# Identity and zero multiplications inserted in TensorE's planned waits, in an attention and rational feed-forward kernel

## The chip, the cores and the metric

The kernel runs on one core of a Trainium2 chip. Its time is the device time of one execution, in microseconds. Before the change the median of three runs is 824.97 us (824.67 to 826.0). The engines are TensorE (PE, with its weight loads as PEld), VectorE (DVE), ScalarE (ACT), GpSimd (POOL), and SyncE (SP), which issues the transfers. [...]

## The reference

Two attention steps and a feed-forward block with a rational function between its two products:

```python
def sm_attn(qq, kk, vv):
    s = scale * np.matmul(qq, kk.transpose(0, 1, 3, 2))
    a = np.exp(s - np.max(s, axis=-1, keepdims=True))
    a = a / (np.sum(a, axis=-1, keepdims=True) + 1e-09)
    return np.matmul(a, vv)
p_packed = sm_attn(p, k, v)                    # 32 packed rows for each head
out = sm_attn(q, p_packed, p_packed)           # 8 x 8 heads, 576 rows, 64 wide
# x: 4608 x 512, the heads side by side
h = x @ w_in                                   # 512 -> 2048
P = a[0] + a[1]*h + a[2]*h**2 + a[3]*h**3
Q = 1.0 + abs(b[0])*abs(h) + abs(b[1])*h**2
out = (P / (Q + 1e-6)) @ w_out                 # 2048 -> 512
```

The weights w_in and w_out come in as 64-bit floats.

## The kernel before, in words

The kernel goes through eight batches of 576 tokens. For each batch `attention` transposes k, forms the scores of the packed rows (buffer `small`), their exponentials (`kx`) and the packed result (`ppT`), transposes q (also into `kx`), forms the second scores, and leaves the normalised weights as two float32r parts, `AH` and `AL`. `m_chunk` multiplies the packed result by w_in (`win`, float32; products in the banks `at`) and splits it into the high and low part `m`. `hidden` multiplies `m` with `AH` and `AL` into the two PSUM banks `h` (six steps of 288 columns for one block) and evaluates the rational function (`U`, `V`, `Y`); `gh` and `gl` are the parts of the result. `accumulate` multiplies them by the parts of w_out (`w`), in steps of 512 columns, into the PSUM banks `acc`.

The weights' 64-bit words have to be turned into float32 first. `convert` does it with two ScalarE passes (lines "m<-m", "w<-w", "win<-m" in the trace) and three VectorE passes per portion, 15 portions and two halves in all, in the first 140 us. While words are left (`early`), `m_chunk` casts its products on ScalarE and forms the low part through a further multiplication by the negative identity (`neg`, in buffer `full`; "m<-full" in the trace), so that VectorE is spared.

Nothing is issued as it is written. `Planner` (line 30) records every instruction with its engine and operands, prices it (`COST`, `F32`), and `schedule` makes a list schedule from the prices. `order` gives the sequence by planned start, and `issue` (line 212) hands the instructions to the engines in that sequence. Each engine then works strictly through its queue, waiting wherever an operand or a buffer isn't ready. Therefore the planned gaps on TensorE set the number of inserted multiplications, while the real gaps are those of the trace. The prices that matter are these:

```python
COST = {"vector": (70, 1.04), "scalar": (93, 0.83), "gpsimd": (215, 2.11), "tensor": (15, 0.417)}
TRANSPOSE, F32 = (15, 0.834), (30, 1.667)
```

They are ns for one instruction and ns for a column. The PSUM banks are two each for `acc`, `h`, `at` and `V`; during the first batch `attention` uses `acc` beside `at`.

Of the kernel before, what the change touches and what calls it, by code (L numbers as in the profile page):

```python
# [14 lines left out]
F32R = mybir.dt.float32r  # L15
# [4 lines left out]
ALU = mybir.AluOpType  # L20
# [3 lines left out]
P = 128  # L24
# [7 lines left out]
class Planner:  # L32
# [156 lines left out]
    def order(self):  # L189
        n = len(self.ops)  # L190
        self.costs = [self.price(*x) for x in self.ops]
        self.transfers = [self.transfer(calls[0][1]) if engine == "sync" else 0 for engine, calls in self.ops]
        before = self.edges()
        after = [[] for _ in range(n)]
        for i, x in enumerate(before):
            for j in x:
                after[j].append(i)
        sync = [x[0] == "sync" for x in self.ops]
        rank = list(range(n))
        best = None  # L200
        for r in range(self.ROUNDS):
            start, end = self.schedule(before, after, rank)
            if best is None or max(end) < best[0]:
                best = self.best = max(end), start, end
            s, e = self.schedule(after, before, [-x for x in end], True)
            m = max(end)
            rank = [m - x for x in e]
        self.t0 = best[1]; self.deps = dict(enumerate(before))
        self.end = best[0]
        return sorted(range(n), key=lambda i: (best[1][i], i))  # L210

    def issue(self):
        for i in self.order():
            engine, calls = self.ops[i]
            for name, args, kwargs in calls:
                getattr(getattr(self.nc, engine), name)(*args, **kwargs)  # L216

# [14 lines left out]
class Ring:  # L232
# [10 lines left out]
    def next(self, shape=None, dtype=None):  # L243
        return self.at(self.used % self.n, shape, dtype)
# [3 lines left out]
def attention_rational_ffn(  # L248
# [12 lines left out]
    B, H, T, D = q.shape  # L261
# [19 lines left out]
    sb = ctx.enter_context(tc.tile_pool(name="sb", bufs=1))  # L281
    ps = ctx.enter_context(tc.tile_pool(name="ps", bufs=1, space=PSUM))
    tc.nc.scalar.preload_act_table_set("natural_log_exp_and_others")
    nc = Planner(tc.nc)


    ident = sb.tile([P, P], F32, name="ident")
    make_identity(tc.nc, ident)
    ab, abS, one, root = (sb.tile([P, n], F32, name=x) for n, x in ((6, "ab"), (7, "abS"), (1, "one"), (5, "root")))
    win = sb.tile([P, NCH, NCC, CF], F32, name="win")  # L290
    G = sb.tile([P, NFC, 2 * REM], F32, name="G")
# [20 lines left out]
    gh_ring, gl_ring = (Ring(sb, x, 2, [P, 2, HMAIN], F32R) for x in ("gh", "gl"))  # L312
    acc_ring = Ring(ps, "acc", 2, [P, DM])
    h_ring = Ring(ps, "h", 2, [P, 512])
    V_ring = Ring(ps, "V", 1, [P, 2, 512])
    at_ring = Ring(ps, "at", 2, [P, 512])


    def constants():
        nc.vector.tensor_scalar(neg, ident, -1.0, None, ALU.mult)  # L320
        nc.sync.dma_start(ab[:, 0:4], a.rearrange("(o n) -> o n", o=1).broadcast_to([P, 4]))
        nc.sync.dma_start(ab[:, 4:6], b.rearrange("(o n) -> o n", o=1).broadcast_to([P, 2]))
        nc.vector.tensor_scalar(abS[:, 0:6], ab, S, None, ALU.mult)
        nc.vector.scalar_tensor_tensor(abS[:, 4:6], abS[:, 4:6], -1.0, abS[:, 4:6], ALU.mult, ALU.max)
        nc.vector.memset(one, (1.0 + 1e-6) * S)

        m, e, p, r, i = (root[:, n : n + 1] for n in range(5))
        nc.vector.scalar_tensor_tensor(m, ab[:, 5:6], -1.0, ab[:, 5:6], ALU.mult, ALU.max)
        nc.vector.tensor_scalar(m, m, 2.0**-126, None, ALU.max)
        nc.vector.tensor_scalar(e.bitcast(I32), m.bitcast(I32), 23, None, ALU.logical_shift_right)  # L330
        nc.vector.tensor_scalar(e.bitcast(I32), e.bitcast(I32), 127, None, ALU.add)
        nc.vector.tensor_scalar(p.bitcast(I32), e.bitcast(I32), 1, 23, ALU.logical_shift_right, ALU.logical_shift_left)
        nc.vector.reciprocal(i, p)
        nc.vector.tensor_scalar(m, m, i, i, ALU.mult, ALU.mult)
        nc.scalar.activation(r, m, AF.Ln)
        nc.scalar.activation(r, r, AF.Exp, scale=0.5)
        nc.vector.reciprocal(i, r)
        nc.vector.scalar_tensor_tensor(r, m, i, r, ALU.mult, ALU.add)
        nc.vector.tensor_scalar(abS[:, 6:7], r, p, 0.5 * S**0.5, ALU.mult, ALU.mult)
        for i, reg in enumerate((reg_a3, reg_b0, reg_b1, reg_root)):  # L340
            nc.scalar.reg_load(reg, abS[0:1, 3 + i : 4 + i].bitcast(I32))
# [8 lines left out]
    words = [("in", 2 * c, 2) for c in range(NCH)] + [("out", 2 * c, 2) for c in range(NCH - 1)]  # L350
# [298 lines left out]
    def m_chunk(bb, c, n=1):  # L649
        assert index["in", 2 * (c + n) - 1] < converted  # L650

        early = converted < len(words)
        f = slice(c % 2 * CF, (c % 2 + n) * CF)
        if c % 2 == 0:
            M[bb, c // 2] = m_ring.at(c // 2)
        m = [M[bb, c // 2][:, i] for i in range(2)]
        t = [at_ring.next()[:, 0 : n * CF] for _ in range(NG)]
        tiles(
            (
                (  # L660
                    t[r][32 * j : 32 * j + 32], PPT[bb][64 * r : 64 * r + 64, r, 32 * j : 32 * j + 32],
                    win[64 * r : 64 * r + 64, c : c + n, j, :],
                ),
                dict(start=True, stop=True),
            )
            for j in range(NJ)
            for r in range(NG)
        )
        for r in range(NG):
            mh, ml = (x[:, r, f] for x in m)  # L670
            if early:
                nc.scalar.copy(mh, t[r])
                nc.tensor.matmul(t[r], neg, mh, start=False, stop=True, skip_group_check=True)
                nc.scalar.copy(ml, t[r])
            else:
                split(t[r], mh, ml, nc.vector)
# [81 lines left out]
    def acc_block(u, i):  # L758
        bb, x, c = units[u]
        if c == 0 and i == 0:  # L760
            ACC[bb, x] = [acc_ring.next() for _ in range(2)]
        gh, gl = GS[bb, x, c]
        acc = ACC[bb, x][i]
        for f in range(2):
            cols = slice(i * P, (i + 1) * P)
            accumulate(acc, gh[:, f, cols], gl[:, f, cols], 2 * c + f, c == 0 and f == 0, c == NCH - 1 and f == 1)
        if c < NCH - 1:
            return
        if i == 0:
            O[bb, x] = o_ring.next()  # L770
        o = O[bb, x]
        ov = out[bb * T : bb * T + NS * P, :].rearrange("(p i x) m -> p x i m", i=2, x=2)[:, x]
        if u == NU - 1 and i == 1:
            nc.vector.tensor_copy(o[:, i, :], acc)
        else:
            nc.scalar.copy(o[:, i, :], acc)
        if u == NU - 1:
            nc.sync.dma_start(ov[:, i, :], o[:, i, :])
        elif i == 1:
            nc.sync.dma_start(ov, o)  # L780

    for what in ("k0", "rem", "k1", "v0", "v1", "q0", "q1"):
        load(0, what)
    constants()
    load_words(2)
    for _ in attention(0):
# [18 lines left out]
    for bb in range(1, B):  # L805
        gen = attention(bb)
        at = [u for u in range(2 * UB * bb - 30, 2 * UB * bb - 3) if u not in mt]
# [4 lines left out]
    def stage(u):  # L812
        if u in pipe:
            next(pipe[u])

    def filler(i):
        if i in mt:
            m_chunk(*mt[i])
        for x in fill.get(i, ()):
            next(x)  # L820

    for u in range(NU + LAG + 2):
        if u < NU:
            pipe[u] = hidden(*units[u])
        stage(u)
        if 0 <= u - LAG < NU:
            acc_block(u - LAG, 0)
        filler(2 * u)
        stage(u)
        stage(u - 2)  # L830
        stage(u - 1)
        for x in rem.get(u, ()):
            remainder(*x)
        convert()
        while converted < len(words) and due(words[converted]) <= u + 1:
            convert()
        if 0 <= u - LAG < NU:
            acc_block(u - LAG, 1)
        filler(2 * u + 1)
    with tc.manual_schedule():  # L840
        nc.issue()


# [26 lines left out]
```

## Time and profile before

| | us |
|---|---|
| median of three runs | 824.97 |
| profiled execution | 823.16 |
| its span, first to last instruction | 821.4 |
| TensorE busy in the span | 774.1 (94%) |
| VectorE busy | 693.6 (84%) |
| ScalarE busy | 691.5 (84%) |
| GpSimd busy | 460.9 (56%) |
| mean granted TensorE clock | 0.969 |

Read the shares by stage, since the averages mix two stages with different limits. The span is cut in 40 slices of some 20.5 us on the profile's page; the granted clock is below 0.9 only in slices 2 to 5 and 7. From about 147 us to the end TensorE is busy without a break. [...]

### The profile page before, as it was taken

Reading aid. Unit: us, or ns where it says so; the run is one execution under the profiler, and the core shown is the slowest. Engines: PE = TensorE matmul, PEld = TensorE weight load, DVE = VectorE, ACT = ScalarE, POOL = GpSimd, SP = SyncE. Lnnn points to the kernel's source line nnn. Section 1 sums busy time; section 2 is a strip of 40 time slices with the busy share of each in tenths; the row PEclk is TensorE's granted clock in tenths of the full one; section 3 lists DMA queues with packets and bytes.
Section 4 is the critical chain, followed back from the end, with each engine's and each line's share of the span. In section 5 each row is a group of like instructions: output and inputs, shape, how many; then the busy total and the mean of one; then the engine's idle time right before and its main releaser. Section 6 shows DMA issues by size and latency. Waiting matters only on the chain.

```text
span 821.4 us, 15529 instructions
## 1 busy us (share of the span) xinstructions
PE 774.1 (94%) x5584; PEld 613.7 (75%) x5584; DVE 693.6 (84%) x1296; ACT 691.5 (84%) x1566; POOL 460.9 (56%) x462
## 2 busy tenths in 40 slices
PE   5677788999999999999999999999999999999997
PEld 3355565888877877788877877788877878778886
DVE  2999999888898788988798778988798788998873
ACT  5898888899797879999888869999888889898872
POOL 0006455755487546755577445755578445856663
PEclk9678798999999999999999999999999999999999
DMA  8973241010400212010400203010400210000001
GB/s 250 387 253 105 104 123 27 26 57 26 123 27 1 81 50 87 27 52 31 123 26 1 81 20 117 27 52 30 123 27 1 77 37 31 26 1 27 26 2 39
DMA packets 50941, 56.06 MB, mean 68 GB/s; under 512 B 13488, under 2 KB 40112, under 8 KB 50864
## 3 DMA queue, kind: packets, MB, share of 16 engines
q1 hardware_dynamic: 50864, 55.07, 20.9%
q8 instruction: 44, 0.72, 0.4%
q14 instruction: 33, 0.27, 0.1%
HBM read 45.62 MB, written 9.44 MB: 67 GB/s over the span
## 4 chain that ended last, share of the span: by engine, by line
PE 75%; DVE 12%; ACT 7%; DMA 2%; issue 1%; SPq 1%; POOL 0%; DVEq 0%; ACTq 0%; POOLq 0%
PE acc L216 36%; PE h L216 23%; PE at L216 16%; DVE Y L216 5%; DVE small L216 3%; DMA m<-in_moe_w_in_dram 2%; DVE w L216 2%; ACT w L216 1%; ACT V L216 1%; ACT m L216 1%; DVE V L216 1%; ACT Y L216 1%; SPq L216 1%; ACT U L216 1%; ACT kx L216 1%
## 5 line engine op out<-in xcount | busy, mean ns | idle before, releaser
L216 PE MATMUL acc<-w,gh 128*128 128x512 f32 x1024 | 330.6, 401 | 4.4 <-ACT w L216 4.4
L216 PEld LDWEIGHTS acc<-w,gh 128*128 128x128 f32 x1024 | 186.6, 190 | 47.8 <-issue 5.8
L216 POOL TENSOR_TENSOR U<-U,sq 128x576 f32<-128x576 f32 x118 | 168.8, 1431 | 73.1 <-ACT U L216 31.6
L216 POOL TENSOR_TENSOR gl<-Y,gh 128x512 fp32r<-128x512 f32 x128 | 166.2, 1299 | 65.0 <-ACT gh L216 32.2
L216 PE MATMUL acc<-w,gl 128*128 128x512 f32 x512 | 198.4, 401 | 0.0
L216 PE MATMUL h<-AH,m 128*128 128x288 f32 x1024 | 193.6, 308 | 4.5 <-DVE Y L216 4.0
L216 PEld LDWEIGHTS h<-AH,m 128*128 128x128 f32 x1024 | 160.0, 192 | 36.2 <-DVE Y L216 16.9
L216 ACT ACTIVATE Y<-h,abS 128x288 f32<-128x288 f32 x256 | 128.2, 513 | 27.6 <-PE h L216 23.8
L216 DVE TENSOR_TENSOR Y<-Y,h 128x288 f32<-128x288 f32 x256 | 111.3, 447 | 40.0 <-ACT sq L216 20.0
L216 DVE SCALAR_TENSOR_TENSOR Y<-Y,abS,V 128x576 f32<-128x576 f32 x128 | 103.4, 808 | 39.3 <-ACT V L216 38.6
L216 DVE SCALAR_TENSOR_TENSOR Y<-Y,abS,h 128x288 f32<-128x288 f32 x256 | 126.4, 507 | 3.3
L216 ACT ACTIVATE sq<-h 128x288 f32<-128x288 f32 x236 | 98.3, 422 | 33.9 <-PE h L216 31.9
L216 PEld LDWEIGHTS acc<-w,gl 128*128 128x128 f32 x512 | 96.7, 190 | 28.4 <-issue 7.7
L216 PE MATMUL h<-AL,m 128*128 128x288 f32 x512 | 112.7, 300 | 0.0
L216 POOL COPY G<-Y 128x64 f32<-128x64 f32 x128 | 34.6, 270 | 135.9 <-DVE Y L216 102.9
L216 ACT ACTIVATE U<-h 128x288 f32<-128x288 f32 x256 | 100.9, 426 | 8.5 <-DVE V L216 6.6
L216 ACT ACTIVATE V<-U,one 128x576 f32<-128x576 f32 x128 | 99.0, 774 | 8.1 <-DVE Y L216 6.5
L216 DVE SCALAR_TENSOR_TENSOR Y<-V,Y 128x576 f32<-128x576 f32 x128 | 96.1, 751 | 2.0
L216 DVE SCALAR_TENSOR_TENSOR V<-U,V 128x576 f32<-128x576 f32 x128 | 96.2, 751 | 0.0
L216 ACT CAST gh<-Y 128x512 fp32r<-128x512 f32 x128 | 82.0, 641 | 5.2 <-DVE Y L216 3.5
L216 ACT ACTIVATE V<-V 128x576 f32<-128x576 f32 x128 | 85.4, 667 | 0.4
L216 PEld LDWEIGHTS h<-AL,m 128*128 128x128 f32 x512 | 84.1, 192 | 0.3
(123 smaller groups left out, 908.3 us busy)
## 6 DMA issues: line engine op xcount, KB each, us to landing
nat<-in_k_dram SPq DMA_DIRECT2D x16, 512.0 KB, 4.0
out_dram<-o SPq DMA_DIRECT2D x15, 512.0 KB, 3.1
w<-in_moe_w_out_dram SPq DMA_DIRECT2D x14, 512.0 KB, 4.4
nat<-in_v_dram SPq DMA_DIRECT2D x14, 512.0 KB, 3.9
nat<-in_q_dram SPq DMA_DIRECT2D x14, 512.0 KB, 5.0
m<-in_moe_w_in_dram SPq DMA_DIRECT2D x8, 512.0 KB, 9.5
w<-in_moe_w_in_dram SPq DMA_DIRECT2D x8, 512.0 KB, 11.0
rkq<-in_k_dram SPq DMA_DIRECT2D x8, 128.0 KB, 4.2
```

Source lines behind the costliest of these rows:

```text
L216: getattr(getattr(self.nc, engine), name)(*args, **kwargs)
```

## The change

Between two planned TensorE instructions `issue` now asks a function `idle` for instructions to insert. If the plan leaves a gap of t ns before an instruction that starts ahead of 150 us, it inserts t/140 of them, at most 24. As long as no hidden block has begun, they are float32 multiplications of the 128x128 identity by itself into a spare PSUM bank (`spare`, one of the two `h` banks). Once one has begun, they are float32r multiplications of a block of zeros (new buffer `zero`, 128x64) by up to 256 columns of the words last used, added to an `acc` or `h` sum that is still open, which stays the same. Where no sum is open nothing is inserted. One VectorE instruction makes the zeros.

```diff
-    def issue(self):
+    def issue(self, idle=None):
+
+        free = 0.0
         for i in self.order():
             engine, calls = self.ops[i]
+            if engine == "tensor":
+                for name, args, kwargs in idle(i, free, self.start[i]):
+                    getattr(self.nc.tensor, name)(*args, **kwargs)
+                free = self.start[i] + self.costs[i]
             for name, args, kwargs in calls:
                 getattr(getattr(self.nc, engine), name)(*args, **kwargs)
...
+    zero = sb.tile([P, D], F32R, name="zero")
...
+    spare = h_ring.at(1)
...
+        nc.vector.tensor_scalar(zero, ident[:, 0:D], 0.0, None, ALU.mult)
...
+    IDLE_COST, IDLE_END = 140, 150e3
+    first_h = min(i for i, (e, x) in enumerate(nc.ops) if e == "tensor" and str(x[0][1][0].tensor.tag).startswith("h"))
+    begun, sums = False, {}
+
+    def idle(i, t0, t1):
+        nonlocal begun
+        todo = []
+        n = min(int((t1 - t0) / IDLE_COST), 24)
+        begun = begun or i == first_h
+        if nc.start[i] < IDLE_END and n > 0:
+            if sums:
+                out, words = list(sums.values())[-1]
+                todo = [("matmul", (out, zero, words), dict(start=False, stop=False, skip_group_check=True))] * n
+            elif not begun and t0 > 0:
+                todo = [("matmul", (spare[:, 0:P], ident, ident), dict(start=True, stop=True))] * n
+        for name, args, kwargs in nc.ops[i][1]:
+            tag = str(args[0].tensor.tag)
+            if name == "matmul" and tag[:1] != "V" and tag[:2] != "at" and args[1].dtype == F32R:
+                n = min(args[0].shape[-1], 256)
+                sums.pop(tag, None)
+                if not kwargs["stop"]:
+                    sums[tag] = (args[0][0:D, 0:n], args[2][:, 0:n])
+        return todo
+
     with tc.manual_schedule():
-        nc.issue()
+        nc.issue(idle)
```

Three places show what it does to TensorE's queue. The numbers behind a buffer's name count its uses and differ between the two kernels where a new buffer shifts them; line 216 of before is line 222 of the changed kernel, and line 219 issues what is inserted.

At the start of the program, TensorE transposes k (`nat`), the packed rows (`pn`) and the last rows (`rkq`). Before:

```order
L216 MATMUL acc_1_89<-ident,nat_1_75 128x128 x4
L216 MATMUL at_1_88<-ident,nat_1_75 128x128 x4
L216 MATMUL acc_3_93<-ident,pn_1_78 128x128 x2
L216 MATMUL acc_2_90<-ident,nat_2_79 128x128 x4
L216 MATMUL at_2_91<-ident,nat_2_79 128x128 x4
L216 MATMUL at_3_92<-ident,rkq_1_76 128x128 x4
```

On TensorE at the same place, now:

```order
L222 MATMUL acc_1_91<-ident,nat_1_77 128x128 x4
L222 MATMUL at_1_90<-ident,nat_1_77 128x128 x4
L219 MATMUL h_1_76<-ident 128x128 x5
L222 MATMUL acc_3_95<-ident,pn_1_80 128x128 x2
L219 MATMUL h_1_76<-ident 128x128 x7
L222 MATMUL acc_2_92<-ident,nat_2_81 128x128 x4
L222 MATMUL at_2_93<-ident,nat_2_81 128x128 x4
L219 MATMUL h_1_76<-ident 128x128 x2
L222 MATMUL at_3_94<-ident,rkq_1_78 128x128 x4
```

Fourteen identities stand between the same transposes in the same sequence.

Some 25 us later TensorE forms the first products with w_in (into the `at` banks) and their corrections by the negative identity (`full`), while ScalarE casts the results between its conversions. Before:

```order
L216 MATMUL at_13_125<-win,ppT_1_87 32x256
L216 MATMUL at_12_124<-m_5_123,full_1_74 128x256
L216 MATMUL at_13_125<-m_5_123,full_1_74 128x256
L216 MATMUL at_14_130<-win,ppT_1_87 32x256
...
L216 MATMUL at_14_130<-m_5_123,full_1_74 128x256
L216 MATMUL at_15_131<-m_5_123,full_1_74 128x256
L216 MATMUL at_16_135<-win,ppT_1_87 32x256
```

On TensorE at the same place, now:

```order
L222 MATMUL at_13_127<-win,ppT_1_89 32x256
L219 MATMUL h_1_76<-ident 128x128 x4
L222 MATMUL at_12_126<-m_5_125,full_1_75 128x256
L219 MATMUL h_1_76<-ident 128x128
L222 MATMUL at_13_127<-m_5_125,full_1_75 128x256
L219 MATMUL h_1_76<-ident 128x128 x20
L222 MATMUL at_14_132<-win,ppT_1_89 32x256
...
L219 MATMUL h_1_76<-ident 128x128 x5
L222 MATMUL at_14_132<-m_5_125,full_1_75 128x256
L219 MATMUL h_1_76<-ident 128x128 x11
L222 MATMUL at_15_133<-m_5_125,full_1_75 128x256
L219 MATMUL h_1_76<-ident 128x128 x16
L222 MATMUL at_16_137<-win,ppT_1_89 32x256
```

Between each product and its correction, and between a correction and the next product, there are now up to 20 identities; the sequence of the others is the same.

Near the end of the conversions TensorE forms the products with w_in for the second batch, 512 columns at a time (banks `at_53` and `at_54`). Before:

```order
L216 MATMUL h_24_288<-AH_1_85,m_6_134 128x288 x4
L216 MATMUL h_24_288<-AL_1_86,m_6_134 128x288 x2
L216 MATMUL at_53_319<-win,ppT_2_144 32x512
L216 MATMUL at_54_320<-win,ppT_2_144 32x512
...
L216 MATMUL acc_13_171<-w_28_265,gh_8_262 128x512
```

On TensorE at the same place, now:

```order
L222 MATMUL h_25_290<-AH_1_87,m_6_136 128x288 x4
L222 MATMUL h_25_290<-AL_1_88,m_6_136 128x288 x2
L219 MATMUL acc_14_174<-w_28_267,zero 64x256 x21
L222 MATMUL at_53_321<-win,ppT_2_146 32x512
L222 MATMUL at_54_322<-win,ppT_2_146 32x512
...
L222 MATMUL acc_13_173<-w_28_267,gh_8_264 128x512
```

Here 21 multiplications of zeros by words of w_out, added to the open sum `acc_14`, stand ahead of the product.

## Rows read from the trace of the kernel before

**Rows 1.** Stretches: length, busy us of PE, PEld, DVE, ACT, POOL (instructions); granted clock; DMA.

```profile
47.58:68.00 20.42, 13.18 (x105) 9.51 (x104) 18.56 (x32) 20.30 (x42) 5.20 (x3) 0.91 0.49 153
68.00:112.00 44.00, 37.00 (x293) 27.21 (x293) 43.78 (x74) 39.05 (x81) 23.00 (x21) 0.81 0.37 123
112.00:121.00 9.00, 7.19 (x42) 4.97 (x39) 9.00 (x19) 7.26 (x17) 5.41 (x5) 1.00 0.35 94
121.00:136.00 15.00, 13.97 (x101) 9.60 (x102) 14.23 (x28) 12.09 (x26) 8.40 (x9) 0.89 0.23 68
147.20:800.00 652.80, 649.23 (x4652) 525.24 (x4652) 557.89 (x1053) 564.07 (x1316) 404.26 (x406) 1.00 0.15 45
```

**Rows 2.** TensorE in order of time, transposes of q: start, us, [idle before <-releaser].

```profile
22.95 1.11 PE L216 MATMUL acc<-ident,w 128*128 128x128 f32 x4 [2.97 <-DMA w<-in_q_dram]
...
24.71 1.92 PE L216 MATMUL acc<-ident,w 128*128 128x128 f32 x8
26.56 0.73 PE L216 MATMUL at<-kx,ppT 64*32 64x288 f32 x16
```

**Rows 3.** Single microseconds, as rows 1; the clock stands behind POOL.

```profile
25.00:26.00 1.00, 1.00 (x7) 1.00 (x6) 1.00 (x3) 0.96 (x4) 0.00 (x0) 0.50 1.05 387
26.00:27.00 1.00, 1.00 (x19) 0.53 (x19) 0.98 (x2) 0.89 (x2) 0.00 (x0) 0.68 1.05 387
139.00:140.00 1.00, 0.00 (x0) 0.00 (x0) 1.00 (x3) 0.77 (x2) 0.00 (x0) 0.64 0.00 0
146.00:147.00 1.00, 1.00 (x7) 0.92 (x7) 1.00 (x4) 0.74 (x3) 0.00 (x0) 0.95 0.00 0
```

**Rows 4.** TensorE in order of time, packed float32 products and what follows them.

```profile
79.50 0.66 PE L216 MATMUL at<-win,ppT 64*32 64x256 f32 x16
80.10 0.50 PE L216 MATMUL acc<-w,gl 128*128 128x512 f32 x1
...
132.28 1.09 PE L216 MATMUL at<-win,ppT 64*32 64x512 f32 x16
133.30 0.73 PE L216 MATMUL acc<-w,gl 128*128 128x512 f32 x2
...
140.72 1.96 PE L216 MATMUL at<-win,ppT 64*32 64x512 f32 x14 [3.33 <-DVE m L216]
```

**Rows 5.** The chain that ended last, 140 to 153 us: start, us, engine, group.

```profile
140.72 1.96 PE at L216 x14
142.68 1.58 PE acc L216 x3
144.25 1.92 PE h L216 x8
...
147.20 5.25 PE acc L216 x23
152.45 0.80 PE h L216 x6
```

**Rows 6.** TensorE in order of time, the first transposes.

```profile
4.74 1.08 PE L216 MATMUL acc<-ident,nat 128*128 128x128 f32 x4 [4.74 <-DMA nat<-in_k_dram]
5.61 1.06 PE L216 MATMUL at<-ident,nat 128*128 128x128 f32 x4
6.54 0.66 PE L216 MATMUL acc<-ident,pn 128*128 128x128 f32 x2
7.29 1.12 PE L216 MATMUL acc<-ident,nat 128*128 128x128 f32 x4
```

**Rows 7.** ScalarE in order of time, the first hidden block's Y.

```profile
47.56 0.50 ACT L216 ACTIVATE Y<-h,abS 128x288 f32<-128x288 f32 x1 [1.43 <-PE h L216]
```

**Rows 8.** Stretches of the first scores and of the products with v.

```profile
9.84:11.40 1.56, 1.47 (x49) 0.73 (x48) 0.73 (x2) 0.41 (x2) 0.00 (x0) 1.00 1.08 375
14.50:16.52 2.02, 1.87 (x82) 1.34 (x81) 0.21 (x2) 1.67 (x3) 0.00 (x0) 1.00 1.03 383
```

**Rows 9.** ScalarE in order of time, about 115 us.

```profile
114.95 0.50 ACT L216 ACTIVATE Y<-h,abS 128x288 f32<-128x288 f32 x1 [1.27 <-PE h L216]
```

**Rows 10.** VectorE in order of time, its idle time from 122 to 136 us.

```profile
128.47 0.45 DVE L216 TENSOR_TENSOR Y<-Y,h 128x288 f32<-128x288 f32 x1 [0.41 <-ACT U L216]
...
135.87 0.43 DVE L216 TENSOR_SCALAR o<-o 128x512 int32<-128x512 int32 x1 [0.34 <-ACT full L216]
```

More of the change, by code (lines that the diff above doesn't have):

```diff
@@ L207, in order @@
             rank = [m - x for x in e]
-        self.t0 = best[1]; self.deps = dict(enumerate(before))
-        self.end = best[0]
+        self.end, self.start = best[0], best[1]
+        self.deps = dict(enumerate(before)); self.t0 = best[1]
         return sorted(range(n), key=lambda i: (best[1][i], i))
-    def issue(self):
+    def issue(self, idle=None):
+        free = 0.0
         for i in self.order():
             engine, calls = self.ops[i]
+            if engine == "tensor":
+                for name, args, kwargs in idle(i, free, self.start[i]):
+                    getattr(self.nc.tensor, name)(*args, **kwargs)
+                free = self.start[i] + self.costs[i]
             for name, args, kwargs in calls:
```

## The prediction

> **What bounds the kernel now.** First I read the busy times by stage [rows 1]. From 147 us on TensorE is the limit: it is busy 649.2 of 652.8 us, at full clock. Before that it isn't. From 47.6 to 68 us ScalarE has no idle time (20.30 of 20.42 us), from 68 to 121 us VectorE has hardly any (43.78 of 44.00, then 9.00 of 9.00), and both convert the 64-bit weights there, among other work. In the same stretches TensorE waits, and its granted clock is 0.91, 0.81 and 1.00 of full speed. Only in the last stage can a faster TensorE shorten the program by itself; ahead of 147 us it matters only where its result is awaited by an engine with nothing else to do. And a TensorE that comes late there holds up ScalarE and VectorE, whose queues are in order, so that the whole rest moves.
>
> Next the clock. The transposes of q start at 22.95 us at half clock: 16 of them take 3.61 us up to the next group, 0.226 us each, so about 0.113 at full clock [rows 2]. The granted clock goes from 0.50 to 0.68 in the stretch 26 to 27 us, after 3 to 4 us of these transposes alone [rows 3]. It falls in the 139 to 140 us stretch (0.64 in its mean), within a wait of 3.33 us, and is back at 0.95 in 146 to 147 us [rows 3, 4]. [...]
>
> **What the change adds.** The order of every engine stays as it was; one small VectorE instruction (the zeros, 128x64) is added at the start, where VectorE has nothing to do. TensorE gets 280 more multiplications: 122 of identity by identity (float32, 128 columns) ahead of the first hidden block, and 158 of zeros by 256 columns of words (float32r): 23 up to the end of that block, 73 up to about 96 us, 62 from there to about 143 us. Their number is the gap of the plan divided by 140 ns.
>
> The price of one. Zeros by words: at full clock 23 accumulation steps of 512 columns take 5.25 us, 0.228 each, and 6 hidden steps of 288 columns 0.80 us, 0.133 each [rows 5]; that is 0.42 ns a column, so 0.12 us for 256, under the 140 ns. Identity by identity: no row of before has a plain float32 multiplication of the whole array. The nearest rows are the packed float32 ones, 8 multiplications side by side, two records each: 16 records of 256 columns take 0.60 us (79.50 to 80.10), 16 of 512 columns take 1.02 us (132.28 to 133.30) [rows 4]. The difference is 0.42 us for 256 columns, 1.64 ns a column or four cycles, so 0.21 us for 128 columns at full clock and 0.42 at half. The low bound is one record only, as a transpose has: 0.113 us [rows 2]. The high bound is half clock throughout, 0.42 us. I take 0.21 us, since a float32 multiplication shows two records and a transpose one. So an identity fill costs half as much again as the plan allots.
>
> [...]
>
> **The first 47 us.** In before TensorE starts at 4.74 us, and the first hidden block is finished at 47.56 us, when ScalarE, idle for 1.43 us, gets it [rows 6, 7]. What TensorE does between, at full clock: 64 transposes at 0.113 are 7.2 us, and 1.1 more for the first ten at half clock, since the first rows show 0.2 us each [rows 6]; 12 hidden steps 1.6 us; 6 corrections of 256 columns 0.7 us; five packed batches of 16 records at 0.60, 3.0 us [rows 4]; the first scores and the first products with v 1.47 and 1.87 us [rows 8]. Together 17 us. The fills in the same stretch: 7 identities at half clock 2.9 us, 115 at 0.21, 24.2 us, 23 zeros 2.8 us; together 29.9 us. 4.74 + 17 + 29.9 = 51.6 us without one wait, against 47.6: TensorE becomes the limit of the start, and ends it at least 4.0 us late. Some waits stay (for the copies of the transposes, for the casts of the products with w_in, for AH): I followed the casts on paper, which alternate with the conversions on ScalarE, and found ScalarE standing idle for one to two microseconds at three of them, because the 13, 20, 11 and 16 identities stand ahead of the very products that it is to cast. I add 1.3 us and take 5.3 us as the lateness at 47.6 us. ScalarE's 1.43 us of idle time there is used up by then.
>
> Is that lateness lost? ScalarE has no reserve from 47.6 to 68 us, and VectorE none from 68 to 121 us [rows 1], so it is carried on. Nothing in these stretches gets faster by a faster TensorE. The zero fills there cost 73 x 0.12 = 8.8 us; TensorE has 7.0 us idle in 68 to 112 us [rows 1], and at a granted clock of 0.81 some 38% of the time is at half, so about 14 us of its work there shrinks by 7 us. They fit: 0 us.
>
> **112 to 136 us.** Around 114 us TensorE is awaited: ScalarE idles 1.27 us for a hidden block [rows 9], ahead of which 2 fills now stand, and 3 more ahead of the transposes behind it: 0.3 us lost of the 0.6. Around 122 to 128 us TensorE is at half clock and on the chain; at full clock it would be some 2 us faster, but VectorE behind it has only 0.41 and 0.34 us of idle time to give [rows 10]: 0.5 us won.
>
> **136 to 147 us.** TensorE waits 3.33 us for VectorE's split of the last product [rows 4], and then works from 140.72 to 147.20 at half clock nearly to the end: 14 packed records, 5 accumulation and 12 hidden steps, 6.48 us [rows 5]. At full clock these are 0.9 + 5 x 0.228 + 12 x 0.133 = 3.6 us. 21 fills ahead of the packed product take 2.5 us of the wait, so the clock should hold; two more fills cost 0.2 us. 2.6 us won, and this counts in full, since from here TensorE is the limit.
>
> **The sum.** 5.3 + 0.3 - 0.5 - 2.6 = +2.5 us. The profiled execution took 823.16 us (span 821.4 and 1.8 around it), so 825.7; the median of the runs shown is 1.8 us above the profiled execution, so 827.5 us.
>
> **Rivals.**
> A, faster: an identity fill takes little more than one record, 0.12 us. Then the start sums to 4.74 + 17 + 14.6 + 0.8 for the first at half + 2.8 = 39.9 us, 7.7 us below 47.6; the fills lie in waits, and only some 0.5 us of lateness is left from places where the plan's gap isn't there on the chip (the 5 and 7 fills at 6.5 and 7.3 us, where before shows no wait [rows 6]). 0.5 + 0.3 - 0.5 - 2.6 = -2.3: 822.7 us. For it: the plan's 140 ns would then be right. Against it: the slope of the packed batches.
> B, no change: the lateness at 47 us is as forecast, but half of it is recovered, because ScalarE and VectorE are only apparently without reserve (a record's duration holds some waiting), so +2.6 and the same gain: 825 us. Against it: only 0.1 us in 20 is left there [rows 1].
> C, much slower: the fills don't raise the clock. Then an identity costs 0.42 and a zero fill 0.23 us, the first stretch carries 51 + 5 us of fills instead of 14 us of waits, and the end moves by about 40 us: 867 us. [...]
>
> **Chances.** Forecast (late by 4 to 7 us at 47 us, so +1 to +5 at the end) 0.60, A 0.20, B 0.16, C 0.04. About 0.2%, 1.65 us, is what a measurement of this kernel can tell from no change. The forecast's lower part falls inside that (0.11 of 0.60), B mostly (0.10, the rest on the faster side with 0.05), A almost all beyond it. Slower 0.52, same 0.22, faster 0.26. The range takes in A's lower edge and the forecast with an identity at 0.24 us (122 x 0.03 = 3.7 us more): 821.8 to 831.3 us.
>
> **What would show it.** In the profile of the changed kernel: the identity group at 0.2 us from start to start (0.12 would be A); two records for each; ScalarE's first Y of the hidden block at about 53 us instead of 47.56; the granted clock at 1.00 from 10 to 50 us and from 139 to 147 us (0.5 there would be C); VectorE without idle time and each of its conversions some 5 us later than before up to 121 us; the last stage of TensorE as long as before, and its start, the packed product at 140.72 us, some 5 us later, with 2.6 us of that given back by 147 us. The forecast is wrong if the first Y comes before 50 us, or if the lateness at 68 us isn't there at 121 us.

## The result and the profile after

The changed kernel takes 827.43 us in the median of 11 runs (825.4 to 831.57), the kernel before 824.86 us in as many (823.32 to 826.0). The ratio is 1.0036, with a 95% interval of 1.0020 to 1.0052: slower by 2.6 us, where 827.5 us were forecast. The two profiled executions stand further apart: 827.43 us with a span of 825.6 against 823.16 us with a span of 821.4, because the profiled execution of before lies 1.7 us under its median and that of the changed kernel on it. It is the 4.2 us between the two spans that the profiles have to explain.

Two stretches of before that [rows 1] doesn't have, the first 43 us of TensorE's work and the end of the conversions (length, busy us of PE, PEld, DVE, ACT, POOL, granted clock, DMA):

```profile
4.74:47.58 42.84, 28.95 (x290) 18.85 (x290) 30.74 (x62) 32.69 (x61) 0.29 (x1) 0.76 0.99 341
136.00:147.20 11.20, 7.87 (x38) 4.74 (x37) 11.09 (x20) 8.26 (x18) 5.24 (x5) 0.70 0.01 1
```

The same stretches of the changed kernel, with those of [rows 1] between them:

```profile
4.74:47.58 42.84, 42.55 (x490) 38.68 (x491) 24.69 (x55) 27.31 (x51) 0.29 (x1) 1.00 0.99 343
47.58:68.00 20.42, 16.50 (x138) 13.00 (x136) 17.16 (x26) 18.13 (x37) 0.30 (x1) 0.92 0.48 147
68.00:112.00 44.00, 38.25 (x361) 30.56 (x360) 43.22 (x70) 39.27 (x83) 20.80 (x19) 0.88 0.29 99
121.00:136.00 15.00, 14.89 (x113) 11.25 (x112) 15.00 (x29) 12.11 (x25) 8.65 (x9) 1.00 0.29 89
136.00:147.20 11.20, 11.05 (x83) 8.46 (x82) 11.04 (x19) 10.31 (x23) 5.33 (x5) 1.00 0.16 48
147.20:800.00 652.80, 649.38 (x4662) 524.62 (x4663) 560.34 (x1061) 565.10 (x1317) 406.02 (x407) 1.00 0.14 45
```

TensorE is busy in 42.55 of the first 42.84 us: it has become the limit of the start. Its clock stands at full there (1.00, in before 0.76), which is what the fills are for, and again from 136 to 147 us (1.00, in before 0.70), while ScalarE got only 27.31 us of work done in the start instead of 32.69. Late in the program all is as before.

The price of an identity stands in TensorE's rows (start, us, group; the next start ends the stretch, since a group's us run past it: 6.52 + 2.34 = 8.86, and the next starts at 8.65):

```profile
6.52 2.34 PE L219 MATMUL h<-ident 128*128 128x128 f32 x10
8.65 0.63 PE L222 MATMUL acc<-ident,pn 128*128 128x128 f32 x2
...
35.70 4.63 PE L219 MATMUL h<-ident 128*128 128x128 f32 x40
40.26 0.66 PE L222 MATMUL at<-win,ppT 64*32 64x256 f32 x16
```

Twenty identities are 40 records and take 4.56 us, 0.114 a record and 0.228 for one; the first five take 2.13 us, 0.43 for one, which is the price at half clock, although the row of that stretch shows 1.00. The plan allots 0.14.

What ScalarE makes of it, up to the first hidden block (answers to [rows 7]; in brackets the idle time before, and what ended it):

```profile
34.40 0.65 ACT L222 CAST m<-at 128x256 fp32r<-128x256 f32 x2 [2.59 <-PE at L222]
...
41.01 0.37 ACT L222 CAST m<-at 128x256 fp32r<-128x256 f32 x1 [1.72 <-PE at L222]
...
49.18 0.37 ACT L222 CAST m<-at 128x256 fp32r<-128x256 f32 x1 [1.62 <-PE at L222]
...
54.98 0.50 ACT L222 ACTIVATE Y<-h,abS 128x288 f32<-128x288 f32 x1 [0.41 <-PE h L222]
```

Three times it waits for a product that stands behind 13, 20 and 16 identities, 5.9 us in all. The first Y comes at 54.98 instead of 47.56 us, 7.4 us late. The waits add up to it: ScalarE was 2.3 us late ahead of the first of them (the conversion that starts at 28.33 us in before starts at 30.59 us), and Y itself now waits 0.41 instead of 1.43 us; 2.3 + 5.9 - 1.0 = 7.2 us.

The end of the conversions, first on TensorE and then in the chain that ended last (answers to [rows 4, 5]):

```profile
143.46 2.62 PE L219 MATMUL acc<-w,zero 128*64 128x256 f32 x21
146.01 1.04 PE L222 MATMUL at<-win,ppT 64*32 64x512 f32 x2
147.36 1.09 PE L222 MATMUL at<-win,ppT 64*32 64x512 f32 x14 [0.31 <-DVE m L222]
```

```profile
146.63 0.69 DVE m L222
147.36 1.09 PE at L222 x14
148.45 0.66 PE acc L222 x2
...
151.63 5.24 PE acc L222 x23
```

From VectorE's split (146.63 us, before 139.99) to the end of the span it takes 679.0 us, before 681.4: the 14 packed records take 1.09 us instead of 1.96, and the accumulation of 23 steps begins 4.3 us after the packed product instead of 6.5 [rows 5]. The change wins 2.4 us there, and has lost 6.6 us by then.

### The profile page after: what moved, and what is told of

Read it like the earlier page. It is cut to its first block, busy times and chain, and to the rows that moved or that the text cites. A ratio compares the mean times of both kernels' runs of the same rounds, so it can differ in the third digit from the quotient of the medians.

```text
span 825.6 us, 16337 instructions
## 1 busy us (share of the span) xinstructions
PE 802.6 (97%) x5986; PEld 651.2 (79%) x5986; DVE 692.7 (84%) x1297; ACT 692.1 (84%) x1566; POOL 458.0 (55%) x462
## 4 chain that ended last, share of the span: by engine, by line
PE 81%; DVE 10%; ACT 6%; issue 1%; POOL 0%; DMA 0%; DVEq 0%; ACTq 0%; POOLq 0%
PE acc L222 38%; PE h L222 22%; PE at L222 17%; DVE Y L222 4%; PE h L219 4%; DVE small L222 2%; DVE w L222 1%; ACT w L222 1%; ACT Y L222 1%; ACT V L222 1%; DVE V L222 1%; ACT U L222 1%; PE acc L219 1%; ACT m L222 1%; DVE o L222 0%
## 5 line engine op out<-in xcount | busy, mean ns | idle before, releaser
L222 PEld LDWEIGHTS acc<-w,gh 128*128 128x128 f32 x1024 | 185.2, 189 | 44.5 <-issue 6.0
L222 PE MATMUL h<-AH,m 128*128 128x288 f32 x1024 | 190.2, 304 | 2.5 <-DVE Y L222 2.2
L222 PEld LDWEIGHTS h<-AH,m 128*128 128x128 f32 x1024 | 157.2, 189 | 31.2 <-DVE Y L222 13.4
L222 POOL COPY G<-Y 128x64 f32<-128x64 f32 x128 | 32.0, 250 | 143.1 <-DVE Y L222 117.9
```

## The experiments

Each kernel was run beside the kernel before on the same chip; the experiments fall in three groups on different chips, so between groups ratios are compared and not times. "First Y" is ScalarE's first step on a hidden block, "split" VectorE's second split of a packed product (139.99 us in before), "rest" what the span has left behind the split. All from the profiled executions but the ratios.

| kernel | ratio to before (95%) | first Y | split | span | rest |
|---|---|---|---|---|---|
| before | 1 | 47.56 | 139.99 | 821.4 | 681.4 |
| the change | 1.0036 (1.0020 to 1.0052) | 54.98 | 146.63 | 825.6 | 679.0 |
| zeros only | 0.9964 (0.9951 to 0.9977) | 46.99 | 140.33 | 819.4 | 679.1 |
| identities only | 1.0105 (1.0088 to 1.0123) | 54.66 | 147.54 | 829.1 | 681.6 |
| identities at 240 ns | 0.9951 (0.9938 to 0.9964) | 46.97 | 139.38 | 818.1 | 678.7 |
| last 52 zeros only | 0.9957 (0.9945 to 0.9969) | 47.65 | 139.38 | 818.6 | 679.2 |
| float32r in place of identities | 0.9962 (0.9946 to 0.9978) | 46.88 | 139.85 | 818.6 | 678.8 |
| only the 21 zeros | 0.9979 (0.9967 to 0.9991) | 48.11 | 140.94 | 820.1 | 679.2 |
| without the first 14 | 1.0035 (1.0019 to 1.0051) | 51.76 | 143.62 | 822.4 | 678.8 |
| 240 ns and last 52 zeros | 0.9981 (0.9968 to 0.9994) | 48.09 | 140.76 | 819.9 | 679.1 |
| first 23 and last 52 zeros | 0.9957 (0.9942 to 0.9972) | 47.65 | 139.94 | 818.7 | 678.8 |
| identities at 240 ns, again | 0.9943 (0.9927 to 0.9960) | 47.13 | 138.78 | 817.6 | 678.8 |

**Zeros only.**

```diff
-            elif not begun and t0 > 0:
+            elif False:
```

> The 122 identity multiplications are left out, the 158 of zeros stay. My theory (identities cost 0.228 us each against 0.14 planned, and make TensorE the limit up to 55 us): the lateness of 7.4 us at ScalarE's first Y goes; the 23 zeros up to there, partly at half clock, cost 1 to 3 us against 1.2 us of idle time, so Y comes at 48 to 50 us; the 2.2 us won around 147 us stay; the end between -2 and +0.5 us against before. Rival (the zeros delay as much as they win, and all inserted work is lost time): slower than before by 1 us or more.

Measured: 3.0 us faster than before (821.19 against 824.16 us), more than expected; the first Y is at 46.99 us, earlier and not later. The lateness goes with the identities, and the rest behind the split is as short as with the change. The rival falls.

**Identities only.**

```diff
-                todo = [("matmul", (out, zero, words), dict(...))] * n
+                todo = []
```

> The 158 multiplications of zeros are left out, the 122 identities stay. Theory: ScalarE's first Y at 52 to 53 us (7.4 us late less the 2.7 us of the 23 zeros), this is carried to 140 us, and nothing is won back around 147 us, since the clock is at half there as in before: +4.5 to +5.5 us against before. Rival (ScalarE and VectorE make the lateness good by 120 us): under +2 us.

Measured: 7.8 us slower than before. The first Y is 7.1 us late, the split 7.55, and the rest as long as in before, so that on balance nothing is made good: the rival falls. My figure was some 3 us too low. I had taken 2.7 us for the 23 early zeros; they are worth 0.3 us of the first Y, since without them TensorE waits there, 0.93 us for a cast and 0.93 us for AH.

**Identities at 240 ns.**

```diff
-                todo = [("matmul", (spare[:, 0:P], ident, ident), dict(...))] * n
+                todo = [("matmul", (spare[:, 0:P], ident, ident), dict(...))] * min(int((t1 - t0) / 240), 24)
```

> As the change, but a planned gap holds one identity for each 240 ns instead of 140: 65 instead of 122. Theory: 57 x 0.228 = 13 us less in the first stretch; TensorE has waits again there, the first Y comes 0.5 to 2.5 us late, of which the gain around 147 us takes 2.2: -2 to +0.5 us against before. Rival (not the price but any fill in the start holds up the chain): half of the change's lateness stays, +1.5 us or more.

Measured: 4.2 us faster than before, and some 7 us faster than the change by the two ratios: 57 identities fewer. It is also 1.2 us faster than zeros only on the same chip (819.68 to 820.75 us against 820.67 to 821.83 us), so that 65 identities win something where 122 lose. The first Y is at 46.97 us, and ScalarE waits for none of the three casts. The clock is at full ahead of the first hidden block (shown below, with both mended).

**The last 52 zeros only.** A counter leaves out the first 106 zeros, and the identities are left out.

```diff
+                made += n
+                if made <= 106:
+                    todo = []
```

> Only the last 52 multiplications of zeros are left (16, 1, 12, 21 and 2, from about 120 us of before on). Theory: up to 120 us all is as in before; the clock is at full from 140.7 to 147 us, and TensorE passes there in 3.9 instead of 6.5 us: -2 to -3 us against before. Rival (the gain there is taken back by VectorE, whose results are awaited next): -0.5 to +0.5 us.

Measured: 3.5 us faster, a little more than expected. The start is as in before (first Y 47.65 us), the split comes 0.6 us earlier, where the prediction put down 0.2 for 112 to 136 us, and the rest is 2.2 us shorter, where it put down 2.6 for 136 to 147 us.

**Float32r in place of the identities.** The same number at the same places, of the negative identity, which is there in float32r.

```diff
-                todo = [("matmul", (spare[:, 0:P], ident, ident), dict(...))] * n
+                todo = [("matmul", (spare[:, 0:P], neg, neg), dict(...))] * n
```

> As the change, with the same 122 early multiplications at the same places, but of the negative identity by itself in float32r (one record of 128 columns in place of two of float32). Theory (the price of a multiplication is what makes the start late): at 0.06 to 0.11 us each they take 7 to 13 us instead of 27.8 and fit the waits, first Y at 47 to 48.5 us, the end -3 to -4.5 us against before, as with identities at 240 ns. Rival (it is the number and the places, each standing ahead of awaited work): Y after 51 us, the end 0 us or later.

Measured: 3.2 us faster than before, first Y at 46.88 us. The 20 fills that stand ahead of the second product with w_in, in TensorE's rows:

```profile
30.84 2.35 PE L219 MATMUL h<-full 128*128 128x128 f32 x20
33.12 1.39 PE L222 MATMUL at<-win,ppT 64*32 64x256 f32 x16
```

2.28 us for 20, 0.114 each, half the price of the identities. With number and places the same, the price decides between 0.36% slower and 0.38% faster. This is the cleanest of the runs on that question.

**Only the 21 zeros** ahead of the packed product near 140 us (`if not 135 < made <= 156: todo = []`, no identities).

> Of all inserted multiplications only the 21 ahead of the packed product at 140.7 us of before are left. Theory (the gain of the zeros is the clock from 140.7 to 147 us, with some 0.6 us from 121 to 136 us): granted clock at full from 139 us on, -2.0 to -3.0 us against before, 0.5 to 1 us less gain than the last 52. Rival (the gain is spread over many fills that hold the clock up earlier): -1 us or less.

Measured: 1.7 us faster. The rest is 679.2 us, the whole 2.2 us of it; the clock is 1.00 throughout 137 to 148 us. The first Y of this execution came 0.55 us late, with nothing changed ahead of it. So one group of 21 gives the gain behind the split. The earlier gain isn't there: between the VectorE rows that answer to 110.78 and 139.99 us of before, this execution loses 0.2 us, at a clock of 0.89 from 121 to 136 us, where that of the last 52 zeros wins 0.9 us at 1.00. The two medians come from different chips, with intervals that just meet, so the difference of 1.8 us between them isn't settled by this.

**Without the first 14 identities** (`if made <= 14: todo = []` for the identities).

> As the change, without the 14 identities ahead of the first scores (5, 7 and 2). Theory (TensorE is the limit from 4.8 to 55 us, so each microsecond taken out of it is won whole): they took 2.13 + 2.0 + 0.45 = 4.6 us, some 1 us of it where the clock would rise later without them; first Y 3 to 4.5 us earlier, at 50.5 to 52 us, and the end 3 to 4.5 us earlier than with the change, -0.5 to -2 us against before. Rival (waits for ScalarE's casts come in their place): under 2 us earlier.

Measured: no gain in the median, 1.0035; its runs fall in two groups, 823.9 to 825.0 us (three, the profiled one among them) and 826.4 to 827.8 us (eight). In the profiled one the first Y is 3.2 us earlier, as expected, and the span 3.2 us shorter. By the median I was wrong; a second trace of this kernel shows more.

> The kernel without the first 14 identities once more, for its trace, since its runs fell in two groups, 823.9 to 825.0 and 826.4 to 827.8 us, and the profiled one in the first. Theory: the groups differ in the first 55 us, where TensorE is the limit: in the slower one the clock rises later or falls once, so that first Y comes some 3 us later, near 55 us. Rival: the first Y is at 51.8 us as in the other and the difference arises after 60 us.

This execution took 827.05 us: first Y at 53.23 us, 1.5 us after the other, split 2.7 us after, the rest 679.0 us. Both theories hold half. Of the first 1.5 us, 0.9 come from transfers: TensorE got k 0.32 us later and waited 0.61 us more for its second half, where the 14 identities would have stood, and as the limit of the start it never made that good. Another 0.5 us I put down to TensorE's clock by the price alone, an estimate, since no row shows the granted clock there: the last four transposes and the first scores take 1.99 us (10.25 to 12.24) instead of 1.48 (9.32 to 10.80), a single score product 0.63 instead of 0.40 us. The other 1.25 us arise behind the first Y. Here is TensorE's clock (length, PE busy, granted clock, DMA) in the first execution and in the second:

```profile
62.00:64.00 2.00, 1.40 (x17) 1.00 0.70 202
64.00:66.00 2.00, 1.11 (x6) 1.00 0.17 60
```

```profile
62.00:64.00 2.00, 2.00 (x11) 0.50 0.00 0
64.00:66.00 2.00, 2.00 (x16) 0.50 0.18 34
```

And ScalarE in the second, which in the first has no idle time there:

```profile
63.42 0.50 ACT L222 ACTIVATE Y<-h,abS 128x288 f32<-128x288 f32 x1 [0.27 <-PE h L222]
64.28 0.59 ACT L222 COPY kx<-at 128x512 f32<-128x512 f32 x1 [0.35 <-PE at L222]
65.72 0.50 ACT L222 ACTIVATE Y<-h,abS 128x288 f32<-128x288 f32 x1 [0.85 <-PE h L222]
```

At half clock the hidden blocks of 63 to 66 us come too late for ScalarE, 1.47 us in all. Nothing is inserted there in any of these kernels, and the level that the clock happens to have decides.

All fourteen traces agree on this place. In before it is the 12 hidden steps and 4 transposes that begin at 55.78 us. From the first start to the last they take 2.00 us in five traces (before, the change, the last 52 zeros, the first one without the first 14 identities, and the second of identities at 240 ns), at a clock of 1.00 and without idle time on ScalarE. In the nine others they take 3.1 to 3.7 us at a mean clock of 0.50 to 0.66, ScalarE idles 0.7 to 1.5 us, and VectorE falls back by 1.0 to 1.9 us. Single spans of two kernels can therefore differ by as much without any difference in what was inserted; what sets the level there wasn't tried.

**The changed kernel once more.**

> The changed kernel once more, for its trace, since its runs go from 825.4 to 831.6 us. Theory: the end moves with the first Y (54.98 us at a span of 825.6), one for one. Rival: the first Y is within 0.5 us of 54.98 and the span differs by more than that.

Measured: 828.68 us, span 826.9: first Y 0.66 us later than in the first execution, split 1.37 us later, span 1.3 us longer. Half of the difference is the first Y; the other half arises at the place above, with the clock at 0.50 from 64 to 66 us and ScalarE idle for 0.85 us. The theory of one for one is too simple.

**Both mended: 240 ns and the last 52 zeros.**

> Identities at one for each 240 ns (65) and of the zeros only the last 52. Theory: the parts are independent; the early identities are worth 0 to -0.6 us and the last zeros -3.5 us: -3.5 to -4.5 us against before, within 0.7 us of identities at 240 ns with all zeros. Rival (the zeros from 69 to 96 us are worth something with the identities): 1 us slower than with all zeros.

Measured: 1.8 us faster, some 2.4 us less than with all zeros. Missed. The profile has 1.1 of the 1.8 us between the two spans in the start. TensorE at identities of 240 ns with all zeros, then without the first 106 of them:

```profile
42.00:44.00 2.00, 1.90 (x17) 1.00 1.05 376
44.00:46.00 2.00, 1.88 (x16) 1.00 1.07 359
```

```profile
42.00:44.00 2.00, 1.21 (x5) 0.70 1.04 378
44.00:46.00 2.00, 1.56 (x7) 0.50 1.06 359
```

Without the 23 early zeros the clock falls at 43 us, just before the first hidden block for which ScalarE idles (1.66 us instead of 0.41), and the first Y comes at 48.09 instead of 46.97 us. From there to the split both take nearly as long (92.67 and 92.41 us), so in these traces the zeros from 69 to 96 us show no worth of their own, and they don't bear the rival out.

**The first 23 and the last 52 zeros**, no identities (`if 23 < made <= 106: todo = []`), **and identities at 240 ns again** on the same chip.

> No identities; of the zeros the 23 up to the first hidden block and the last 52. Theory (mended after the runs so far: the clock matters in the start too, at one place, from 44 to 47.6 us, where ScalarE idles for the first hidden block; the 23 zeros raise it there): clock at full from about 43 us, first Y at 47 us, 0.6 to 1.1 us before the kernels without these zeros; end -3.5 to -4.5 us against before. Rival (they only take time): Y at 47.6 us or later, end -3 us or less gain.

> The same kernel as identities at 240 ns, on the chip of this call, to stand beside early and last zeros: -3.5 to -4.5 us against before; 0 to 0.7 us faster than early and last zeros, since its clock is at full from 10 us on but ScalarE and VectorE set the pace between. Rival (the identities are what brings it): 1 us or more faster.

Measured: 3.5 us (820.33) and 5.0 us (818.84) faster than before. The first is at the lower end of what I expected, and its first Y was not early (47.65 us): the clock is at half until some 44.5 us (0.86 in the mean of 44 to 46 us), so that the zeros ahead of the block run at half clock, 0.21 us each (6 in the 1.28 us from 40.70 us), and ten of the block's twelve steps, then at full clock, begin only at 45.59 us. In the trace of zeros only, the same program up to this point, the clock rose 1.0 us earlier and Y came at 46.99 us; so a difference of that size can lie between two executions. With the identities at their price the first Y is 0.5 us earlier; the clock was at full from 36 to 48 us in the first trace of that kernel (1.00 in every 2 us). The two intervals overlap, so that the order of these two isn't shown; identities at 240 ns with all zeros has the lowest median of its group both times, and beats both kernels of the case.

## Why the prediction was right, and where its sizes were off

The direction, the place and the mechanism are shown: it is the identities (zeros only against identities only), it is their price (float32r at the same places), and the lateness passes through the conversions, with only 0.8 us of it made good ahead of the split. Three VectorE rows of before, and those of the changed kernel that answer to them:

```profile
76.39 1.26 DVE L216 TENSOR_SCALAR small<-small 128x2 f32<-128x2 f32 x1
...
110.78 0.34 DVE L216 TENSOR_SCALAR small<-at,small 128x128 f32<-128x128 f32 x1
...
139.99 0.68 DVE L216 TENSOR_TENSOR m<-at,m 128x512 fp32r<-128x512 f32 x1
```

```profile
83.80 1.25 DVE L222 TENSOR_SCALAR small<-small 128x2 f32<-128x2 f32 x1
...
118.24 0.34 DVE L222 TENSOR_SCALAR small<-at,small 128x128 f32<-128x128 f32 x1
...
146.63 0.68 DVE L222 TENSOR_TENSOR m<-at,m 128x512 fp32r<-128x512 f32 x1
```

7.41, 7.46 and 6.64 us late.

- The price, 0.21 us: measured 0.228, which is 0.009 more in each record than the slope of the packed products gives. The transposes in [rows 2] had shown it: 0.113 for a record of 128 columns, so 0.226 for two. Of the forecast's "four cycles" the rows show only that 1.64 ns a column is 3.9 times the 0.42 ns of float32r [rows 5]. The plan's own price for a float32 multiplication, 30 + 128 x 1.667 = 243 ns, was near too; the 140 ns of the change don't use it.
- The first term, 5.3 us: measured 7.4. On TensorE from 4.79 to 54.98 us the identities take 29.5 us (27.1 forecast), the zeros 3.0 (2.8), the other work 17.3 (17), and its idle time is 0.35 us. So the 1.3 us that I added for waits on TensorE weren't there, and the identities were short by 2.4 us. ScalarE's waits on paper were short too, 5.9 us at three casts where I wrote one to two each.
- The zeros from 69 to 96 us, 0 us: held; 7.42 us late at the first Y, 7.46 behind them.
- 112 to 136 us, 0.2 us won: 0.8 us were won up to the split (7.46 us late ahead of it, 6.64 at it). I had capped the gain by VectorE's idle time in [rows 10], 0.75 us, and taken off fills that turned out to cost nothing. That it takes the zeros isn't shown: the trace of identities only, without a zero, has its clock at 1.00 there too and wins 1.0 us between the same rows (8.52 us late, then 7.55).
- 136 to 147 us, 2.6 us won: 2.4 measured, between 2.2 and 2.7 in every profile of a kernel that keeps the 21 zeros, and none in the one that has only identities.
- The sum by profiles is +4.2 us against +2.5 forecast. That the median fits to 0.1 us is luck: the profiled execution of before, from which I reckoned, lay 1.7 us under its median and made up for a first term that was 2.1 us too small.
- "Nothing in these stretches gets faster by a faster TensorE" was wrong. ScalarE's lack of idle time from 47.6 to 68 us belongs to an execution whose clock was up at the blocks from 55.78 us on. Where it is at half there, 1.0 to 1.9 us are lost, and at 44 us some 1.1. So the clock is worth something at two more places than I named, and early identities at their price, 1.2 us faster than none, are worth it too.
- Rival A had the right condition with the wrong number: at 0.114 us a fill the same change is faster, by 3.2 us (2.3 forecast). Rival B falls by the rows above, where nothing is recovered up to 118 us. Rival C falls, since the clock stands at 1.00 in the first stretch above and an identity costs 0.228 us there, not 0.42 (only the first ones, by their price, were still at half).

What stays open is why the changed kernel's runs spread over 6 us while those of identities at 240 ns spread over 1 to 3 (and those with float32r over 5.8, by one run at 824.84 us). The pairs of traces show two sources, the start at a TensorE without reserve, and the clock's level at the blocks some 8 us behind the first Y; whether these are all wasn't tried.

## What to carry to other kernels

Inserted work was free here only as long as it fitted the wait: 122 multiplications made the first Y 7.4 us late at 0.228 us each, and as many at the same places not late (46.88 us) at 0.114. Price it by its own type from a stream of the same kind (here 20 float32 multiplications are 40 records, 20 of float32r are 20), and count the whole stretch, real work and fills together, against the time that the stretch has. A wait in a plan is not a wait on the chip (5 and 7 identities came where before shows none [rows 6]), and in front of a result that an engine with a full queue awaits, fills that were too long cost nearly their whole excess here (of 7.4 us at the first Y 6.6 were left at the split). Look for the few places where the engine that sets the pace idles for TensorE at half clock: here one group of 21 multiplications near 140 us makes the kernel 1.7 us faster by itself, and with the other 259 it is 2.6 us slower.

## What the runs showed of the hardware

In the first 181 single microseconds of before the granted clock is 1.00 in 121, 0.50 in 44 and between the two in 16. With 21 multiplications by zeros in the wait of 3.33 us [rows 4] it stayed at 1.00 from 137 to 148 us (only the 21 zeros), where that of before is 0.50 in each microsecond from 140 to 146 us. A float32r multiplication of 128 columns takes 0.114 us in a stream, where its columns alone would take 0.054 at the 0.42 ns that longer ones show [rows 5]; and a float32 record of 128 columns takes the same 0.114. For the zeros, 256 columns behind a load of 64, it is 0.121 (21 in the 2.55 us up to the next group), near the 0.108 that the columns would make. So with 128 columns of float32r something beside the columns sets the pace; what it is wasn't tried.
